# Group 4's gate and value rows as seven products, with the first product copied into the second's PSUM bank

## The chip, the cores and the metric

The kernel runs on one core of one Trainium2 chip. The metric is the device time of one execution in microseconds. TensorE multiplies matrices into PSUM (eight banks of 128 x 512 float32), VectorE (DVE) and ScalarE (ACT) read and write PSUM and SBUF, GpSimd (POOL) works in SBUF alone, and SyncE (SP) issues DMA transfers; POOL issues some too.

## The reference, cut to what matters

```python
for t in range(S):                      # B, H, S, D = 4, 8, 768, 64
    state = gamma * state + k[t] (outer) v[t]
    y[t] = scale * q[t] @ state
x   = y, as 3072 tokens x 512
xn  = x / sqrt(mean(x * x) + 1e-6) * rms_g
g   = xn @ w_gate                       # 512 x 1536
val = xn @ w_val                        # 512 x 1536
out = (silu(g) * val) @ w_out           # 1536 x 512
```

Inputs and output are float32; the kernel multiplies in bfloat16 and sums in float32.

## The kernel before, in words

The 768 time steps are cut into six chunks of 128, and each chunk with its four batches makes a group c = 0 to 5 of 512 tokens. A step of the work is a word with indices, such as `A.2.0` (attention scores of chunk 2, batch 0 and 1) or `g.4.3.4.0.4` (gate row block 3 of group 4, for batches 0 to 3), and `ORDER` (L17 to L105) lists every step of the kernel in the order in which it is issued. The loop at L784 walks through the list and calls the function of each word. A letter behind `@` is the engine (D, A, P, S for DVE, ACT, POOL, SP), digits behind `/` are PSUM banks. Each engine works through its own instructions in the list's order; an instruction waits, with all that stands behind it on that engine, until its inputs are there and its output's buffer is free. So the list alone sets the order of the work.

For each chunk and batch the steps are: loads `Lq`, `Lk`, `Lv` (L317), casts and scalings `Cq`, `Ck`, `V` (L348 to L373), transposes on TensorE (`Tq`, `Tk` with copies `Eq`, `Ek`) or by DMA (`tq`, `tk`), scores `A` (L410; `P` for a pair of batches), the causal mask `M0`, `M1` into `am` (L436), the output `Y` (L447), the state sums `K`, `U`, `B`, and the norm: `S` (squares, ACT, L464), `R` (two small POOL instructions, L476) and `N` (DVE, L488). `X` and `XE` transpose the result into `xnT[c]`, 128 x 4 x 512 tokens.

The feed-forward part of a group has 12 row blocks of 128 hidden rows. An ordinary block takes four matmuls of 512 columns for the gate (`g`, L564), four for the value (`v`), a silu by ACT into `sg` (`s`, L574) and a product by DVE into `hT` (`h`, L586).

The down product of each group is made with seven products instead of eight block products, a scheme of Strassen's kind: hidden rows and tokens are cut in halves, `z1` to `z4` (L633) and `w1` to `w4` (L618) are the sums of blocks that go in, and `product` (L652) adds products 1, 6, 7 and 4 in a bank `a`, product 2 in `b`, products 5 and 3 in `c`. Between them `q1`, `q6`, `q7` (`keep`, L666) copy the running sum of `a` out to SBUF (`sn`). `r1` to `r4` (`result`, L675) form the four quarters: `b` + q1, `c` + q7, `c` + q6, and `a` itself. `s1` to `s4` store them.

Group 5's gate and value rows are made with seven products too. `gS1` to `gS4` and `vS1` to `vS4` (`lsum`, L703) are the sums of weight blocks, `X1` to `X4` (`xsum`, L721) those of `xnT`. `rows7` (L737) makes a product for four row blocks (index r = 0 to 2): four matmuls of 256 columns. `gq`, `vq` copy the running sum (`rkeep`, L755), `gr`, `vr` add (`rsum`, L759), `gs1` to `gs4` are silus (`gsilu`, L767), and `h.5...` forms the products for two row blocks and half of the tokens at once. The sums `S3` overwrite blocks of the weights in place, so they come after the last ordinary use of those blocks.

Buffers are rings of slots: `ring` (L221) opens a tile in the next free one of `bufs` slots. `done` keeps the tiles by name.

Of the kernel before, what the change touches and what calls it, by code (L numbers as in the profile page):

```python
# [818 lines left out]
```

## Time and profile before

| | before |
|---|---|
| runs | 226.31, 226.47, 226.80 us (median 226.47) |
| span of the profiled execution | 225.2 us |
| TensorE busy | 216.6 us, 96% of the span |
| VectorE busy | 180.7 us, 80% |
| ScalarE busy | 108.0 us, 48% |
| GpSimd busy | 156.2 us, 69% |
| granted TensorE clock, mean | 1.000 |

The profiled execution's own time is its span, from the first to the last instruction; the time of a run contains what lies around it as well, 1.1 to 1.6 us by the three runs. An engine's busy time is the union of its instructions. The ends of matmuls are modelled, so that a matmul's duration is longer than the distance to the next one. In the views, a row of the table of groups gives the number of instructions behind an x, then busy time and mean duration in ns, then the idle time just before them with what ended it.

### The profile page before, as it was taken

The numbers are of one execution on the slowest core, as the hardware profiler recorded it, in microseconds if no ns is written. First come the engines' busy times: TensorE is split into PE (matmuls) and PEld (weight loads), VectorE is DVE, ScalarE is ACT, GpSimd is POOL, SyncE is SP. The second block draws the span as 40 slices with busy tenths as digits, with TensorE's granted clock in tenths as the row PEclk, the third lists the DMA queues.
The fourth block names the chain that finished last, engine by engine and source line by source line (L and its number), as shares of the span: only waits on it lengthen the run. The fifth ranks groups of instructions, "written<-read, shape, count | busy, mean of one in ns | idle before, by whom it ended". The sixth has DMA issues, their size and how long they took to land.

```text
span 225.2 us, 5544 instructions
## 1 busy us (share of the span) xinstructions
PE 216.6 (96%) x2119; PEld 145.5 (65%) x2119; DVE 180.7 (80%) x322; ACT 108.0 (48%) x261; POOL 156.2 (69%) x210
## 2 busy tenths in 40 slices
PE   8999999999999999999999999999999999999793
PEld 2568775674655884456754667545466888888582
DVE  7497778889978976995939967969979978899562
ACT  6676543643465883474415153213752375663130
POOL 8999998839985578537599983496066499609900
PEclk9999999999999999999999999999999999999999
DMA  6999999999999999885999698596405103000235
GB/s 100 187 178 190 173 177 189 197 209 227 209 158 211 182 198 153 187 204 130 203 135 242 143 254 169 109 200 160 140 4 141 48 0 139 5 0 3 93 138 188
DMA packets 108187, 33.64 MB, mean 149 GB/s; under 512 B 94465, under 2 KB 108161, under 8 KB 108162
## 3 DMA queue, kind: packets, MB, share of 16 engines
q1 hardware_dynamic: 84690, 25.70, 52.6%
q0 software_dynamic: 23472, 7.60, 30.7%
q8 instruction: 16, 0.26, 0.5%
q14 instruction: 9, 0.07, 0.1%
HBM read 28.31 MB, written 6.29 MB: 154 GB/s over the span
## 4 chain that ended last, share of the span: by engine, by line
PE 74%; DVE 10%; POOL 8%; issue 3%; DMA 1%; SPq 1%; ACT 1%; POOLq 0%; ACTq 0%; DVEq 0%
PE g_ps L564 20%; PE v_ps L564 20%; PE a L660 12%; PE c L660 5%; DVE hT L586 3%; DVE z L633 3%; PE b L660 2%; PE a_ps L418 2%; PE y_ps L456 2%; DVE vf L762 2%; PE y_ps L460 2%; POOL vp L329 2%; PE ga L750 2%; PE va L750 1%; DMA out_dram<-r 1%
## 5 line engine op out<-in xcount | busy, mean ns | idle before, releaser
L574 ACT ACTIVATE sg<-g_ps 128x512 bf16<-128x512 f32 (+2 forms) x64 | 35.5, 569 | 57.6 <-PE g_ps L564 46.5
L564 PE MATMUL v_ps<-xnT,wv_b 128*128 128x512 bf16 (+2 forms) x296 | 59.5, 339 | 0.0
L564 PE MATMUL g_ps<-xnT,wg_b 128*128 128x512 bf16 (+2 forms) x296 | 59.0, 339 | 0.2 <-ACT sg L574 0.2
L586 DVE TENSOR_TENSOR hT<-sg,v_ps 128x512 bf16<-128x512 bf16 (+2 forms) x64 | 40.8, 649 | 14.6 <-ACT sg L574 8.3
L564 PEld LDWEIGHTS <-wg_b 128*128 128x128 bf16 x296 | 25.7, 98 | 22.3 <-DVE xnT L152 0.3
L564 PEld LDWEIGHTS <-wv_b 128*128 128x128 bf16 x296 | 25.7, 98 | 21.8
L660 PEld LDWEIGHTS <-hT 128*128 128x128 bf16 x288 | 28.0, 98 | 5.1
L483 POOL TENSOR_SCALAR ms<-ssq 128x1 f32<-128x1 f32 x24 | 5.5, 230 | 28.2 <-ACT xsq L473 27.4
L660 PEld LDWEIGHTS <-z 128*128 128x128 bf16 x216 | 20.8, 98 | 5.7 <-DVE z L633 2.4
L441 DVE TENSOR_TENSOR am<-a_ps,causal 128x512 bf16<-128x512 f32 x32 | 20.5, 683 | 2.2 <-PE a_ps L418 2.1
L497 DVE SCALAR_TENSOR_TENSOR xn<-y_ps,rstd,g_bc 128x512 bf16<-128x512 f32 x22 | 16.4, 748 | 5.4 <-POOL rstd L485 5.2
L556 POOL CAST st_b<-st_f 64x256 bf16<-64x256 f32 x40 | 19.2, 481 | 2.2 <-DVE st_f L549 0.9
L473 ACT ACTIVATE xsq<-y_ps 128x512 bf16<-128x512 f32 x22 | 13.2, 599 | 13.8 <-PE y_ps L460 12.0
L633 POOL TENSOR_TENSOR z<-z,hT 128x512 bf16<-128x512 bf16 x14 | 17.4, 1246 | 2.9 <-DVE z L633 2.5
L660 PE MATMUL a<-wo_b,hT 128*128 128x256 bf16 x144 | 17.7, 273 | 0.0
L633 POOL TENSOR_TENSOR z<-hT 128x512 bf16<-128x512 bf16 x7 | 8.6, 1226 | 10.6 <-PE a L660 7.7
L485 POOL TENSOR_TENSOR rstd<-ms,mhalf 128x1 f32<-128x1 f32 x24 | 13.9, 580 | 2.0
L633 POOL TENSOR_TENSOR hT<-hT 128x512 bf16<-128x512 bf16 x11 | 13.7, 1254 | 2.2 <-PE b L660 2.1
L354 POOL TENSOR_TENSOR qb<-qf,ydec 128x512 bf16<-128x512 f32 x10 | 11.6, 1162 | 4.0 <-DMA qf<-in_q_dram 4.0
L152 ACT COPY sn<-a 128x512 f32<-128x512 f32 x14 | 8.1, 584 | 13.0 <-PE a L660 11.0
L371 ACT ACTIVATE vp<-vf,vdec 128x64 bf16<-128x64 f32 x56 | 14.0, 341 | 0.0
L683 DVE TENSOR_TENSOR r<-c,sn 128x512 f32<-128x512 f32 (+1 forms) x13 | 8.4, 646 | 4.0 <-PE c L660 2.2
(161 smaller groups left out, 392.4 us busy)
## 6 DMA issues: line engine op xcount, KB each, us to landing
out_dram<-r SPq DMA_DIRECT2D x21, 256.0 KB, 2.3
kf<-in_k_dram SPq DMA_DIRECT2D x18, 256.0 KB, 4.0
qf<-in_q_dram SPq DMA_DIRECT2D x16, 256.0 KB, 3.9
vf<-in_v_dram SPq DMA_DIRECT2D x16, 256.0 KB, 4.0
wo_b<-in_moe_w_out_dram POOLq DMA_DIRECT2D x3, 512.0 KB, 8.6
qb<-in_q_dram POOLq DMA_DIRECT2D x8, 128.0 KB, 6.3
vp<-in_v_dram POOLq DMA_DIRECT2D x8, 128.0 KB, 6.7
kb<-in_k_dram POOLq DMA_DIRECT2D x6, 128.0 KB, 6.1
```

Source lines behind the costliest of these rows:

```text
L354: e.tensor_tensor(out=u["qb"], in0=u["qf"], in1=ydec[:, c, :, None].to_broadcast([128, H, D]), op=ALU.mult)
L371: ACT.activation(u["vp"][:, h], u["vf"][:, h], AF.Copy, scale=vdec[:, c, h:h + 1])
L441: DVE.tensor_tensor(out=u["am"][:, i], in0=u["a"][i], in1=m, op=ALU.mult)
L473: ACT.activation(xsq, flat(u["y"]), AF.Square, accum_out=u["ssq"])
L485: POOL.tensor_tensor(out=u["rstd"], in0=ms, in1=mhalf, op=ALU.pow)
L497: DVE.scalar_tensor_tensor(out=u["xn"], in0=flat(u["y"]), scalar=u["rstd"], in1=g_bc, op0=ALU.mult, op1=ALU.mult)
L556: POOL.tensor_copy(st_b[b][r, :, i * 64:i * 64 + 64], st_f[b][r])
L564: nc.tensor.matmul(p[:, (n - n0) * m:(n - n0 + 1) * m], W[w][0][:, s, n * 128:(n + 1) * 128], xnT[c][:, s, b0 * C:b1 * C], start=s == 0, s ...
L574: ACT.activation(sg[:, :cols], done["wg", c, n0, b0][:, :cols], AF.Silu)
L586: DVE.tensor_tensor(out=h_of(c, r)[:, i:i + n1 - n0, b0 * C:b1 * C], in0=sg, in1=p, op=ALU.mult)
L633: e.tensor_tensor(out=x, in0=a, in1=b, op=how)
L660: nc.tensor.matmul(done[x, c][:, q], left(i, c, r)[:, k, q * C:q * C + C], right(i)[:, r, k], start=first and q == r == k == 0, stop=r == ...
```

## The change

Five things are changed.

- Group 4's gate and value rows go through `rows7` like group 5's: `ga1.4.0` and so on replace `g.4...`, `v.4...` and `s.4...`. The sums of weights are now made per r (two k blocks at once, 512 elements) instead of per k (three r at once, 768 elements): 24 sums instead of 16. `X1` to `X4` are made for groups 4 and 5.
- The first product's copy (`q1`, and `gq1`, `vq1`) goes into the PSUM bank of `b`, opened by that copy, and product 2 is added there. The bank must have been written in full by matmuls before (`whole`, and `every` for tiles that write all of a bank). The sum of `b` and q1 falls away: `r1` is a copy (any engine), `gr1` and `vr1` are gone; silu and `h` read the bank of `b` itself.
- `r2` and `r3` (also `gr`, `vr`) are written over the kept copy in `sn`, not into a buffer of their own.
- Rings: `o_sb` 5 to 3, `sn` 4 to 6, `qb` 6 to 5, `kb` 8 to 6, `vp` 8 to 6, `qT` and `kT` 6 to 5, `am` 6 to 3, `sg` 3 to 4, `vf` 6 to 5. The squares of the norm go into the tile `xn`, which `N` then fills.
- The list of steps is a new one, from the third line on.

```diff
-    HB, OB, KD, SN = 6, 5, 12, 4
+    HB, OB, KD, SN = 6, 3, 12, 6
+    QB, KB, VP, KT, AM, SG, VF = 5, 6, 6, 5, 3, 4, 5
...
-    def bank(i, shape, dtype, name):
+    whole = {}
+
+    def bank(i, shape, dtype, name, every=False, seed=False):
+
+        assert not seed or whole[i]
+        whole[i] = every
         return psum.tile(shape, dtype, name=name, tag=f"bank{i}")
...
-        first = i in (1, 2, 5) and r0 == 0
+        first = i in (1, 5) and r0 == 0
...
-    def keep(i, e, c):
-        done["q", i, c] = ring([128, 2, HM], F32, "sn", SN)
-        copy(e, done["q", i, c], done["a", c])
+    def keep(i, e, bk, c):
+        if i == 1:
+            x = done["b", c] = bank(bk[0], [128, 2, HM], F32, "b", every=True, seed=True)
+        else:
+            x = done["q", i, c] = ring([128, 2, HM], F32, "sn", SN)
+        copy(e, x, done["a", c])
...
-    QUARTER = {1: ("b", 1, 0, 0), 2: ("c", 7, 1, 1), 3: ("c", 6, 0, 1), 4: ("a", None, 1, 0)}
+    QUARTER = {1: ("b", None, 0, 0), 2: ("c", 7, 1, 1), 3: ("c", 6, 0, 1), 4: ("a", None, 1, 0)}
...
-    def lsum(w, i, e, k):
+    def lsum(w, i, e, r):
...
-        if i == 4 and w == "v":
-            done["wv", c, 4 * r + 2, 0] = p.rearrange("p n t -> p (n t)")
-
-    def rkeep(w, i, e, c, r):
-        done[w + "q", i, c, r] = ring([128, 2, HM], F32, "sn", SN)
-        copy(e, done[w + "q", i, c, r], done[w + "a", c, r])
+        if i in (2, 4) and w == "v":
+            done["wv", c, 4 * r + (2 if i == 4 else 0), 0] = p.rearrange("p n t -> p (n t)")
+
+    def rkeep(w, i, e, bk, c, r):
+        if i == 1:
+            x = done[w + "b", c, r] = bank(bk[0], [128, 2, GT // 2], F32, w + "b", every=True, seed=True)
+        else:
+            x = done[w + "q", i, c, r] = ring([128, 2, HM], F32, "sn", SN)
+        copy(e, x, done[w + "a", c, r])
...
-        x, q = {1: ("b", 1), 2: ("c", 7), 3: ("c", 6)}[i]
-        y = sb.tile([128, H, D], F32, name="vf", tag="vf", bufs=6).rearrange("p h d -> p (h d)")
-        DVE.tensor_tensor(out=y.rearrange("p (n t) -> p n t", n=2), in0=done[w + x, c, r], in1=done[w + "q", q, c, r],
-                          op=ALU.add)
+        y = done[w + "q", {2: 7, 3: 6}[i], c, r]
+        DVE.tensor_tensor(out=y, in0=done[w + "c", c, r], in1=y, op=ALU.add)
```

Of the new list, the front, the place of the output weights, and the beginning of group 4's rows:

```diff
-Lv.0.1@P wg.0.2 wv.0.2 H.1/2 mk1 Eq.0.0@A Tq.0.1/3 Tk.0.1/5 Ek.0.1@A Eq.0.1@D A.0.0/1720 Tq.0.2/4 yd Eq.0.2@A Tq.0.3/3
-M0.0.0 Lv.0.3@P Eq.0.3@A M1.0.0 M0.0.1 M1.0.1 GE@A J.0.0/5 A.0.2/17 wv.2.4 Y.0.0/4 wg.2.4 H.3/2 H.1/3 M0.0.2 Tk.0.3/0
-M1.0.2 K.0.2/6 wv.4.6 S.0.0 D.0.0@D R.0.0 Y.0.2/2 J.0.1/1 Y.0.1/3 J.0.2/7 Ek.0.3@A J.0.3/0 N.0.0 D.0.1@D S.0.2 X.0.0/5
-K.0.0/7 XE.0.0@D wg.4.6 S.0.1 R.0.2 R.0.1 N.0.2 N.0.1 A.0.3/41 g.0.0.2.0.1/5 U.0.2@A X.0.2/6 Lk.1.2@P v.0.0.2.0.1/2
...
+Lv.0.1@P wg.0.2 wv.0.2 H.1/2 mk1 Eq.0.0@A Tq.0.1/3 Tk.0.1/5 Ek.0.1@A wg.4.6 Tq.0.2/4 Eq.0.1@D A.0.0/0253 M0.0.0
+Lv.0.3@P M1.0.0 wg.2.4 J.0.2/7 Eq.0.2@A A.0.2/40 M0.0.2 M1.0.2 yd GE@A Y.0.0/6 S.0.0 R.0.0 H.1/1 J.0.1/2 Y.0.2/1 S.0.2
+H.3/0 M0.0.1 M1.0.1 R.0.2 K.0.2/7 Y.0.1/5 wv.2.4 S.0.1 Tq.0.3/3 D.0.1@D Tk.0.3/2 R.0.1 N.0.0 Lk.1.1@S X.0.0/6 N.0.2
+K.0.1/4 J.0.0/1 XE.0.0@D X.0.2/6 Ek.0.3@A Eq.0.3@A wv.4.6 U.0.2@D J.0.3/7 v.0.0.2.0.1/2 XE.0.2@A N.0.1 Lq.1.3@P
...
+XE.1.2@A z2.0.0@P wo.4.8 v.0.6.7.0.4/5 g.1.11.12.0.4/0 h.0.7.8.0.4 vS1.1@P g.1.6.7.0.4/2 vS2.1@P s.1.6.7.0.4
...
+z2.0.1@D s.1.5.6.0.4 v.1.5.6.0.4/7 h.1.5.6.0.4 Cq.2.2@D Cq.2.1@P s.1.2.3.0.3 Lq.2.0@S w1@D w2@D g.1.9.10.0.4/1
+s.1.9.10.0.4 tq.2.2 s.1.8.9.0.4 v.1.10.11.0.4/0 g.1.0.1.0.3/6 h.1.10.11.0.4 Ck.2.0@D V.2.1@A B.1.2 v.1.8.9.0.4/4
...
+v.3.9.10.0.4/4 tq.5.1 r3.2 X1.4@P B.4.0 X2.4@P Ck.5.2@A ga1.4.0/0 gq1.4.0@A/5 s2.2@S h.3.9.10.0.4 v.3.0.1.0.4/2
+ga6.4.0 gb2.4.0 gq6.4.0@A va1.4.0/4 gS3.0@P ga7.4.0 X4.4@P h.3.0.1.0.4 Lv.5.0@S gS3.1@D gc5.4.0/1 gq7.4.0@D gr2.4.0
+Lv.5.3@S vq1.4.0@A/2 vb2.4.0 gs1.4.0 h.4.0.2.0.2 s.3.4.5.0.4 va6.4.0 v.3.4.5.0.4/5 h.3.4.5.0.4 V.5.3@P vS3.0@P
```

More of the change, by code (lines that the diff above doesn't have):

```diff
@@ L249, in H_ @@
     def H_(e, bk, n):
-        p = bank(bk[0], [128, 4, 128], F32, "hot_ps")
+        p = bank(bk[0], [128, 4, 128], F32, "hot_ps", every=True)
         for _ in range(n):
@@ L349, in Cq @@
         u = t[c, b]
-        u["qb"] = ring([128, H, D], BF16, "qb", 6)
+        u["qb"] = ring([128, H, D], BF16, "qb", QB)
         if c == 0:
@@ L364, in V @@
         u = t[c, b]
-        u["vp"] = ring([128, H, D], BF16, "vp", 8)
+        u["vp"] = ring([128, H, D], BF16, "vp", VP)
         if c <= 1:
@@ L453, in Y @@
             return
-        u["y"] = y = bank(bk[0], [128, H, D], F32, "y_ps")
+        u["y"] = y = bank(bk[0], [128, H, D], F32, "y_ps", every=True)
         for h in range(H):
@@ L465, in S_ @@
         u = t[c, b]
-        xsq = ring([128, DM], BF16, "xsq", 1)
+        xsq = u["xn"] = ring([128, DM], BF16, "xn", 4)
         if "ys" in u:
@@ L489, in N @@
         u = t[c, b]
-        u["xn"] = ring([128, DM], BF16, "xn", 4)
         if "ys" in u:
@@ L560, in ffn @@
         m = (b1 - b0) * C
-        p = done[w, c, n0, b0] = bank(bk[0], [128, GT], F32, w[1] + "_ps")
+        p = done[w, c, n0, b0] = bank(bk[0], [128, GT], F32, w[1] + "_ps", every=n1 - n0 == 1 and m == GT)
         for n in range(n0, n1):
@@ L677, in result @@
         if ("r", i, c) not in done:
-            done["r", i, c] = sb.tile([128, 2, HM], F32, name="r", tag="o_sb", bufs=OB)
+            done["r", i, c] = done["q", q, c] if q else sb.tile([128, 2, HM], F32, name="r", tag="o_sb", bufs=OB)
         s = slice(0, 2) if p is None else slice(p, p + 1)
@@ L732 @@
         for w in "gv":
-            F["%sS%d" % (w, i)] = lambda e, bk, k, w=w, i=i: lsum(w, i, e, k)
+            F["%sS%d" % (w, i)] = lambda e, bk, r, w=w, i=i: lsum(w, i, e, r)
     PLACE = {1: (0, 0), 2: (1, 1), 3: (0, 1), 4: (1, 0)}
     def rows7(w, x, i, bk, c, r):
-        first = i in (1, 2, 5)
+        first = i in (1, 5)
         if first:
-            done[w + x, c, r] = bank(bk[0], [128, 2, GT // 2], F32, w + x)
+            done[w + x, c, r] = bank(bk[0], [128, 2, GT // 2], F32, w + x, every=True)
         p = done[w + x, c, r]
@@ L745, in rows7 @@
                 if i in (1, 2, 4):
-                    l = side(w, *((0, 0), (0, 1), (1, 1))[i // 2], k)
+                    l = side(w, *((0, 0), (0, 1), (1, 1))[i // 2], r)
                 else:
-                    l = done["S", w, {3: 4, 5: 1, 6: 2, 7: 3}[i], k]
+                    l = done["S", w, {3: 4, 5: 1, 6: 2, 7: 3}[i], r]
                 m = part(c, *((0, 0), (1, 0), (1, 1))[i - 1]) if i <= 3 else done["X", {4: 4, 5: 1, 6: 2, 7: 3}[i], c]
-                nc.tensor.matmul(p[:, q], l[:, r, q], m[:, k], start=first and q == k == 0, stop=q == k == 1,
+                nc.tensor.matmul(p[:, q], l[:, k, q], m[:, k], start=first and q == k == 0, stop=q == k == 1,
@@ L767, in gsilu @@
     def gsilu(i, c, r):
         h0, t0 = PLACE[i]
-        x = done["ga", c, r].rearrange("p n t -> p (n t)") if i == 4 else done["gr", c, 4 * r + 2 * h0, 2 * t0]
-        sg = done["s", c, 4 * r + 2 * h0, 2 * t0] = sb.tile(
-            [128, H, D], BF16, name="kb", tag="kb", bufs=8).rearrange("p h d -> p (h d)")
+        x = done["gr", c, 4 * r + 2 * h0, 2 * t0] if i in (2, 3) else done[{1: "gb", 4: "ga"}[i], c, r].rearrange(
+            "p n t -> p (n t)")
+        sg = done["s", c, 4 * r + 2 * h0, 2 * t0] = ring([128, GT], BF16, "sg", SG)
```

213 lines of the change are left out of this document (104 added, 109 removed).

## The prediction

> **What bounds the kernel now.** I read the page first: busy time by engine, then the chain that ended last.
>
> ```profile
> span 225.2 us, 5544 instructions
> ...
> PE 216.6 (96%) x2119; PEld 145.5 (65%) x2119; DVE 180.7 (80%) x322; ACT 108.0 (48%) x261; POOL 156.2 (69%) x210
> ...
> PE 74%; DVE 10%; POOL 8%; issue 3%; DMA 1%; SPq 1%; ACT 1%; POOLq 0%; ACTq 0%; DVEq 0%
> ```
>
> The three runs lie at 226.31 to 226.8 us, median 226.47. The profiled execution is known by its span of 225.2 us, so about 1.27 us lie around it, and I add them to every span below. TensorE is busy for 96% of the span and owns 74% of the chain, so matmul time taken out is worth its full price wherever TensorE has no holes. Next I read the table of busy time by stretch, around the place where the change acts, and TensorE's instructions in order of time at the holes.
>
> ```profile
> 12.00:40.00 28.00, 27.41 (x374) 19.18 (x373) 23.54 (x42) 15.79 (x37) 26.01 (x43) 1.00 1.78 182
> ...
> 156.00:166.00 10.00, 9.23 (x84) 5.14 (x83) 8.24 (x15) 5.36 (x15) 1.48 (x5) 1.00 0.33 93
> ...
> 166.00:176.00 10.00, 10.00 (x85) 5.96 (x83) 9.56 (x17) 4.11 (x10) 6.59 (x9) 1.00 0.41 106
> ...
> 196.00:210.00 14.00, 13.54 (x123) 11.65 (x120) 13.65 (x21) 5.48 (x10) 6.86 (x5) 1.00 0.05 18
> ...
> 146.00:210.00 64.00, 62.38 (x518) 45.31 (x516) 56.55 (x85) 29.68 (x62) 40.99 (x42) 1.00 0.30 79
> ...
> 157.27 0.38 PE L418 MATMUL a_ps<-qT,kT 64*128 64x128 bf16 x7 [0.33 <-DVE r L683]
> ...
> 157.86 0.40 PE L418 MATMUL a_ps<-qT,kT 64*128 64x128 bf16 x8 [0.21 <-DVE hT L586]
> ...
> 158.49 0.81 PE L564 MATMUL g_ps<-xnT,wg_b 128*128 128x512 bf16 x3 [0.23 <-ACT sg L574]
> ...
> 192.40 0.60 PE L750 MATMUL gc<-xnT,kf 128*128 128x256 bf16 x4 [0.39 <-DVE vf L762]
> ...
> 209.17 0.61 PE L660 MATMUL c<-w,z 128*128 128x256 bf16 x4 [0.46 <-DVE z L633]
> ...
> 210.92 1.27 PE L660 MATMUL a<-w,z 128*128 128x256 bf16 x10 [0.92 <-DVE z L633]
> ```
>
> The columns after the length of a stretch are busy PE, PEld, DVE, ACT, POOL, then the granted clock (1.00 throughout), DMA share and GB/s. From 146 us to the end of the seven-product work the six marked holes add up to 2.54 us, and five of the six name DVE as the releaser. A hole is longer than shown, because the ends of matmuls are modelled: the table of groups gives 273 ns for one matmul of 256 columns, while twelve start within 1.31 us (below), 109 ns each, so some 0.16 us hide in each mean. Six times 0.16 and 2.54 make 3.5 us of holes. DVE is the second engine here: 56.55 of 64 us, and 13.65 of 14 in the stretch where TensorE begins to wait.
>
> **The change part by part.**
>
> *TensorE.* These are two pieces of the chain, and rows of the table of groups with shapes kept apart.
>
> ```profile
> 115.21 2.59 PE g_ps L564 x12
> ...
> 178.47 1.31 PE ga L750 x12
> ...
> L660 PE MATMUL a<-wo_b,hT 128*128 128x256 bf16 x144 | 17.7, 273 | 0.0
> ...
> L750 PEld LDWEIGHTS <-wg_b 128*128 128x128 bf16 x48 | 4.7, 98 | 0.5
> ...
> L586 DVE TENSOR_TENSOR hT<-sg,v_ps 128x512 bf16<-128x512 bf16 x52 | 35.0, 682 | 11.5 <-ACT sg L574 7.3 <-PE v_ps L564 3.8
> ...
> L586 DVE TENSOR_TENSOR hT<-kb,vf 128x512 bf16<-128x512 bf16 x9 | 8.4, 945 | 0.2
> ...
> L762 DVE TENSOR_TENSOR vf<-vc,sn 128x512 f32<-128x512 f32 x6 | 4.1, 686 | 0.1
> ...
> L683 DVE TENSOR_TENSOR r<-b,sn 128x512 f32<-128x512 f32 x6 | 4.1, 684 | 1.4 <-PE b L660 1.4
> ...
> L152 ACT COPY sn<-a 128x512 f32<-128x512 f32 x14 | 8.1, 584 | 13.0 <-PE a L660 11.0 <-issue 1.1 <-DVE r L683 0.8
> ...
> L772 ACT ACTIVATE kb<-vf 128x512 bf16<-128x512 f32 x9 | 5.7, 633 | 3.2 <-DVE vf L762 3.2
> ...
> L715 DVE TENSOR_TENSOR qf<-qf,wg_b 128x768 bf16<-128x768 bf16 x2 | 1.9, 970 | 0.0
> ...
> L633 POOL TENSOR_TENSOR z<-z,hT 128x512 bf16<-128x512 bf16 x14 | 17.4, 1246 | 2.9 <-DVE z L633 2.5
> ```
>
> Twelve matmuls of 512 columns take 2.59 us, 0.216 each; group 4's gate and value rows are 2 x 12 blocks of 4, 96 of them, 20.7 us. As seven products they are 2 x 3 x 7 x 4 = 168 matmuls of 256 columns at 1.31/12 = 0.109 us, 18.3 us. That removes **2.4 us**. The weight load of 98 ns stays under the 109 ns of its predecessor, as it does in group 5's rows already. No other matmul is added: counted in both lists, products, attention and warm-up matmuls are the same in number, so 2.4 us is the whole of TensorE's gain.
>
> *The seed.* The first product's copy q1 (row sn<-a, 584 ns on ACT) now goes into the PSUM bank in which the second product then adds. It replaces a copy of the same size into SBUF: 18 of them, six for the down products, six for group 5's rows, and six new ones for group 4's. No row shows an engine writing PSUM. ACT's reads of a whole bank lie between 584 and 633 ns, and I take 584; I see no reason to exclude a gain (say 0.1 each, a copy of 256 columns being the only thing that is shorter) and bound it above by doubling, 1.17 us. On ACT, at 48%, even doubling costs 18 x 0.58 = 10 us of an idle half. What is new is that the second product waits for the copy. In the list at least one other product or 512-wide block (0.44 to 0.87 us) stands between q1 and b2 almost everywhere, and the third product had to wait for the same copy already, so I book nothing; without that cover it is up to 0.6 us a time.
>
> *DVE over the whole kernel.* What goes: 12 ordinary hT (682 ns), group 5's six sums gr1 and vr1 and the six r1 (684 ns each; r1 is a plain copy now, four on ACT, two on DVE). What comes for group 4: 12 sums r2 and r3 (686), 12 hT of which six read both factors from SBUF (945) and six the value from PSUM (684). That is -8.2 -4.1 -2.7 +8.2 +9.8 = +3.0, less 0.8 because three of group 5's hT take their value from PSUM. Copies and casts that the new list puts on DVE instead of ACT or POOL (sorted by the letter behind the @) bring some 5 more, the finer weight sums (24 of 512 elements, not 16 of 768; 970 ns was a dear one) save 1.8. About +5.4 on 180.7.
>
> *DVE where it matters.* I take the stretch of the list from group 4's first gate matmul to the last hT of group 5. TensorE in it, by the two rates: before 96 x 0.216 + 368 x 0.109 + 2.9 of attention = 63.8 us; after 8 x 0.216 + 516 x 0.109 + 2.9 = 61.0. DVE by the means of the rows: before 84 instructions, 59.9 us (hT 20.1, sums r2/r3/r1 of rows 12.4, kept copies 1.4, weight sums 4.5, z 6.9, attention and the rest 14.6); after 92, 65.6 us (hT 21.5, row sums 16.5, kept copies 4.9, weight sums 1.0, z 8.6, the rest 13.1). Back to back the instructions overlap:
>
> ```profile
> 10.65 3.68 DVE L441 TENSOR_TENSOR am<-a_ps,mask 128x512 bf16<-128x512 f32 x6
> ...
> L441 DVE TENSOR_TENSOR am<-a_ps,mask 128x512 bf16<-128x512 f32 x16 | 10.1, 683 | 0.7 <-PE a_ps L418 0.7
> ```
>
> Six take 3.68 us, 0.613 each against a mean of 683 ns, so each counts 0.07 less when the queue is full: 54.0 us before, **59.2 after**, against 61.0 of TensorE. DVE goes from 85% of TensorE's work to 97%. It just does not become the bound by itself, but it has no room left: every wait in its queue, for a silu of 633 ns or a copy of 584 ns from ACT, is passed on, because behind the waiting hT or sum stand the next evictions, and TensorE waits for their banks. In the two stretches above where DVE was at 95% or more (24 us), TensorE lost nothing in one, and 0.46 plus the 0.92 right behind it in the other, with 0.16 twice 1.7 us, 7%. So the holes of the new 61.0 us lie between 0 and 4.3 us; I take 3.8, near the end that the longer stretch gives. Before they were 3.5: **+0.3**.
>
> *The front.* The list is new from the first chunk on. On POOL's queue wv.2.4 and wv.4.6 now stand behind the norm steps R.0.0 and R.0.2 (and R.0.1), where before only wg.4.6 stood behind one. And the last chunk of the output weights, which w1, the first weight sum on DVE, needs whole, is issued later.
>
> ```profile
> L485 POOL TENSOR_TENSOR rstd<-ms,mhalf 128x1 f32<-128x1 f32 x24 | 13.9, 580 | 2.0
> ...
> L483 POOL TENSOR_SCALAR ms<-ssq 128x1 f32<-128x1 f32 x24 | 5.5, 230 | 28.2 <-ACT xsq L473 27.4
> ...
> 40.41 0.81 POOL L345 DMA_DIRECT2D wo_b<-in_moe_w_out_dram  x1
> ...
> 54.29 1.02 DVE L618 TENSOR_TENSOR w<-wo_b 128x1536 bf16<-128x1536 bf16 x1
> ...
> wo_b<-in_moe_w_out_dram POOLq DMA_DIRECT2D x3, 512.0 KB, 8.6
> ```
>
> One R costs 0.81 us of POOL's queue; in return R.0.0 no longer stands behind the two value chunks. The last wo issue began at 40.41 and w1 at 54.29, 13.9 us later. In the new list 8.4 us of matmuls (by the rates above) lie between wo.4.8 and w1, against 0.8 for the issue and 8.6 to land: w1 may wait 1.0 us at the head of DVE's queue, with w2, a cast of k, a scaling of q and two hT of group 1 behind it, whose PSUM banks TensorE wants back. Bounds: from -0.8 (the first norm comes one R's worth earlier, and nothing else is late) to +1.8 (0.8 + 1.0, all of it seen); I take **+0.4**, near the middle, since DVE has room there.
>
> *Smaller rings* (am 6 to 3, kb and vp 8 to 6, o_sb 5 to 3, and others by one). An instruction that opens a slot waits for the last reader of the old tile. Before, no row names such a wait of any weight. Where I followed am, the tightest, one tile (M0.2.1) opens in the list before Y.2.2 has read the tile three back; Y.2.2 follows two steps later, so this is half a microsecond of DVE at the worst. I book zero; what it comes to otherwise belongs to the holes.
>
> Sum: 225.2 - 2.4 + 0.3 + 0.4 = 223.5, and 1.27 around it: **224.8 us**.
>
> **The rivals.**
>
> *DVE falls behind (slower).* The hT products with both factors in SBUF are the ones that swing:
>
> ```profile
> L586 DVE TENSOR_TENSOR hT<-kb,vf x9: 681/692/1647, 187.6 to 207.0; 128x512 bf16<-128x512 bf16 x9
> ```
>
> (least, median, longest). There were 9, there will be 12, spread over two groups in which POOL makes sums too. If all came at the longest, DVE would gain 12 x (1.647 - 0.945) = 8.4 us. The forecast has DVE at 59.2 of 61.0 + 3.8 = 64.8 us, 91%. At that share a quarter of the 8.4 (2.1) makes 67.1 us of stretch, 2.3 more than forecast: 227.1. Half makes 69.4: 229.4. I call it 228.0. It decides against the change once the holes are over 5.5 us (3.5 + 2.4 - 0.4), that is from 1.5 us more DVE work than I sum. For it: 97% of TensorE's work, and 1647 in the row. Against: the median of 692, and POOL's work in the stretch falls (by the rows 42 to 35 us, 16 z sums instead of 20).
>
> The Trainium skill (SBUF — State Buffer, Who interferes with whom) has it that a VectorE instruction with two SBUF inputs and a GpSimd instruction that reads SBUF exclude each other, the second waiting for the whole of the first. By that rule alone, each of the 12 behind a whole POOL sum of 1.25 us, DVE would need some 71 us and the kernel would end near 238, an estimate; the trace agrees that it happens (1647 ns) but for few of the nine.
>
> *The front eats it.* With the whole 1.8 us at the front: 224.8 - 0.4 + 1.8 = 226.2, no difference to speak of. For it: POOL 26.01 of 28 us busy from 12 to 40, so its queue hands on every delay. Against: TensorE idles there for only 0.6 us of 28.
>
> *The holes close.* A new list can also bring the z sums and banks in time. With holes of 1.3 us instead of 3.8: 222.3. For it: the 166 to 176 stretch, full on both engines. Against: less DVE room than before.
>
> **How the numbers follow.** About 0.2% (0.45 us) is what a measurement of this kernel can tell from no change. Forecast 0.58, its own range 223.5 to 226.0; DVE behind 0.23; the front 0.09; holes closed 0.10. Faster 0.58 + 0.10 = 0.68, the same 0.09, slower 0.23. The range runs from 222.5, which leaves out half of the closed holes, to 227.9, which leaves out half of the rival that is slower.
>
> **What would show it.** Right: 248 instead of 296 matmuls each at L564's gate and value, 336 instead of 168 256-wide row products, twelve of them still starting within 1.31 us; DVE near 186 us busy and above 90% from group 4's rows on; holes there naming DVE, 3 to 4.5 us in sum; the first gate matmul within half a microsecond of before. Wrong: a wait of a b product on its seeding copy of more than 0.3 us many times; TensorE waiting for weights before 40 us, or w1 idle in front of wo for over 1 us; hT with a mean well over 1 us; or a long wait of DVE or SP for a ring slot.

## The result, and the profile after

The changed kernel takes 230.48 us (median; the profiled execution 228.72), the kernel before on the same chip 226.58 (226.31 to 226.8): a ratio of 1.0154, interval 1.0122 to 1.0187. It is slower by 1.5%, where 224.8 us, faster than before, was forecast. Ratios, here and below, leave out single runs that fell into a slower state (here the one of 232.92 us) and are not the quotients of the medians. In three later series the same kernel came to 1.0249, 1.0200 and 1.0229 (below). The profiled execution is the fastest of its four, so the profile shows less than the whole loss.

The page after, its span, busy times and chain:

```profile
span 226.8 us, 5721 instructions
...
PE 216.0 (95%) x2191; PEld 152.9 (67%) x2191; DVE 185.8 (82%) x331; ACT 117.6 (52%) x277; POOL 162.8 (72%) x221
...
PE 72%; DMA 10%; POOL 7%; DVE 7%; issue 2%; ACT 1%; SPq 1%; POOLq 0%; DVEq 0%; ACTq 0%
```

The reader should see one thing: DMA owns 10% of the chain, where it owned 1%. DVE, which the forecast watched, owns less than before (7% after 10%). The table by stretch says where. First before, then after; the columns are as in the prediction.

```profile
60.00:150.00 90.00, 89.84 (x819) 55.36 (x817) 70.80 (x121) 42.81 (x120) 62.75 (x89) 1.00 0.91 180
...
150.00:210.00 60.00, 58.38 (x500) 43.46 (x498) 54.65 (x81) 29.15 (x62) 37.19 (x37) 1.00 0.27 72
```

```profile
60.00:150.00 90.00, 87.01 (x819) 55.61 (x818) 73.87 (x121) 44.17 (x121) 69.04 (x91) 1.00 0.91 179
...
150.00:212.00 62.00, 60.17 (x585) 51.76 (x584) 55.93 (x90) 35.85 (x70) 34.70 (x41) 1.00 0.29 78
```

From 60 to 150 us TensorE stood idle for 0.16 of 90 us before; now it does for 2.99. From 150 us on it is idle for 1.8 of 62 us, where it was for 1.6 of 60 before. The waits of TensorE in the changed kernel, largest first (total, times, longest):

```profile
PE a_ps L427 <- DMA qT<-qb: 1.6, 3, 0.9
PE b L670 <- DVE b L156: 1.2, 1, 1.2
...
PE g_ps L572 <- DVE xn L505: 0.5, 1, 0.5
PE va L758 <- POOL wv_b L724: 0.4, 1, 0.4
...
PE y_ps L469 <- POOL st_b L564: 0.3, 1, 0.3
PE g_ps L572 <- DMA xnT<-xn: 0.3, 1, 0.3
```

None of the waits for a DMA is in the list of before. To compare whole kernels I add up, from the start of each matmul to the next, what goes beyond the streaming of its columns (0.216 us for 512, 0.109 for 256, 0.034 for a score product). Us, from one profile each; the first column is the streaming itself:

| kernel | streaming | holes 0–60 | 60–150 | 150–end | span |
|---|---|---|---|---|---|
| before | 211.4 | 4.6 | 0.3 | 3.8 | 225.2 |
| after | 209.0 | 5.6 | 4.3 | 3.1 | 226.8 |
| after, again (first series) | 209.0 | 5.2 | 6.4 | 3.1 | 228.4 |
| after, control of the second series | 209.0 | 5.6 | 5.3 | 3.0 | 227.6 |
| after, control of the third series | 209.0 | 5.2 | 6.8 | 3.0 | 228.8 |
| seed copy on ScalarE | 209.0 | 5.9 | 7.4 | 4.3 | 231.3 |
| after with group 4 plain | 211.4 | 5.2 | 6.2 | 5.5 | 233.0 |
| loads by need | 209.0 | 5.1 | 5.2 | 3.0 | 227.0 |
| down weights early | 209.0 | 5.8 | 6.9 | 3.3 | 229.7 |
| both | 209.0 | 5.4 | 4.6 | 3.9 | 227.6 |
| both, and value sum early | 209.0 | 5.5 | 4.0 | 2.4 | 225.6 |
| and near casts first | 209.0 | 5.6 | 4.6 | 2.5 | 226.3 |
| and two places more | 209.0 | 5.7 | 3.9 | 2.7 | 226.1 |

The account of the profiled execution: streaming -2.4, front +1.0, middle +4.0, late -0.7, together +1.9; the spans differ by 1.6, since what lies before the first and behind the last matmul differs too. The middle is also what varies: 4.3, 6.4, 5.3 and 6.8 us in four profiles of one kernel, while the late part stays at 3.0 to 3.1. (Three runs below, those with the old list put back and with transposes by need, are not in the table: 12 to 19 matmuls are missing from their traces.)

### The profile page after: what moved, and what is told of

The parts are those of the page before. It is cut to its first block, busy times and chain, and to the rows that moved or that the text cites. A ratio compares the mean times of both kernels' runs of the same rounds, so it can differ in the third digit from the quotient of the medians.

```text
span 226.8 us, 5721 instructions
## 1 busy us (share of the span) xinstructions
PE 216.0 (95%) x2191; PEld 152.9 (67%) x2191; DVE 185.8 (82%) x331; ACT 117.6 (52%) x277; POOL 162.8 (72%) x221
## 4 chain that ended last, share of the span: by engine, by line
PE 72%; DMA 10%; POOL 7%; DVE 7%; issue 2%; ACT 1%; SPq 1%; POOLq 0%; DVEq 0%; ACTq 0%
PE g_ps L572 15%; PE v_ps L572 14%; PE a L670 10%; PE c L670 5%; PE va L758 4%; PE ga L758 4%; DMA xnT<-xn 3%; DMA qT<-qb 3%; PE hot_ps L261 3%; PE b L670 2%; PE a_ps L427 2%; PE vc L758 2%; POOL x L735 2%; PE gc L758 2%; DMA kf<-in_k_dram 2%
## 5 line engine op out<-in xcount | busy, mean ns | idle before, releaser
L572 PE MATMUL g_ps<-xnT,wg_b 128*128 128x512 bf16 (+2 forms) x248 | 47.6, 331 | 0.9 <-DVE xn L505 0.5
L572 PE MATMUL v_ps<-xnT,wv_b 128*128 128x512 bf16 (+2 forms) x248 | 48.3, 331 | 0.0
L582 ACT ACTIVATE sg<-g_ps 128x512 bf16<-128x512 f32 (+2 forms) x52 | 28.1, 562 | 32.4 <-PE g_ps L572 23.9
L594 DVE TENSOR_TENSOR hT<-sg,v_ps 128x512 bf16<-128x512 bf16 (+2 forms) x52 | 32.4, 640 | 12.6 <-ACT sg L582 6.4
L572 PEld LDWEIGHTS <-wg_b 128*128 128x128 bf16 x248 | 21.0, 98 | 18.7 <-issue 1.4
L572 PEld LDWEIGHTS <-wv_b 128*128 128x128 bf16 x248 | 21.1, 98 | 16.7 <-DVE xn L505 0.3
L482 ACT ACTIVATE xn<-y_ps 128x512 bf16<-128x512 f32 x22 | 13.1, 595 | 12.8 <-PE y_ps L469 6.3
L643 POOL TENSOR_TENSOR z<-hT,z 128x512 bf16<-128x512 bf16 x10 | 12.7, 1274 | 2.3 <-PE c L670 2.1
L696 DVE TENSOR_TENSOR sn<-c,sn 128x512 f32<-128x512 f32 (+1 forms) x13 | 8.4, 644 | 2.9 <-PE c L670 2.6
L772 DVE TENSOR_TENSOR sn<-gc,sn 128x512 f32<-128x512 f32 x12 | 8.1, 684 | 3.0 <-PE gc L758 2.9
```

Of the source, the lines that this page charges most:

```text
L482: ACT.activation(xsq, flat(u["y"]), AF.Square, accum_out=u["ssq"])
L572: nc.tensor.matmul(p[:, (n - n0) * m:(n - n0 + 1) * m], W[w][0][:, s, n * 128:(n + 1) * 128], xnT[c][:, s, b0 * C:b1 * C], start=s == 0, s ...
L582: ACT.activation(sg[:, :cols], done["wg", c, n0, b0][:, :cols], AF.Silu)
L594: DVE.tensor_tensor(out=h_of(c, r)[:, i:i + n1 - n0, b0 * C:b1 * C], in0=sg, in1=p, op=ALU.mult)
L643: e.tensor_tensor(out=x, in0=a, in1=b, op=how)
```

## The experiments

Theory after the result (ORDER; LATE LOADS and MIDDLE are its narrower forms): the seven products bring what was forecast, and the new list loses it between 60 and 150 us, because tiles that are needed soon stand in the in-order queues behind work for tiles that are needed late. Rivals: PRODUCTS (the copies and sums, or the seeded banks, cost it), RINGS (the smaller rings).

**First series.** *The changed kernel again*, no edit.

> The changed kernel once more, on the chip of the next three. Its four runs so far lie from 228.7 to 232.9 us while the kernel before keeps within 0.5 us, and its profiled run was the fastest of them. Theory ORDER (transfers reach their readers too late in the new list) and theory RINGS (smaller rings hold transfers back) both expect a spread of more than 1 us again and, in a profile of a run near 230 us, more TensorE holes between 30 and 150 us than the 4.7 us of the first profile, released by DMA. Theory DVE (VectorE falls behind in the rows of groups 4 and 5) expects the added holes after 150 us.

Measured 231.89 us (230.31 to 233.56) against 226.45, ratio 1.0249 (1.0189 to 1.0308). The loss is real and its size varies. In its profile the late holes are those of the first one (3.1 us) and the middle ones grow to 6.4, so the theory DVE of the expectation, which put the added holes behind 150 us, falls.

*Old places for the preparation.* The loads, casts and q/k transposes of groups 2 to 5 go to the places that they have in the old list, measured by TensorE's work ahead of them:

```
- ... M1.2.2 M0.2.2 tq.2.1 a6.0.0.3 Lk.4.2@S ...
+ ... M1.2.2 M0.2.2 a6.0.0.3 ...      (128 words Lq, Lk, Lv, Cq, Ck, V, tq, tk moved)
```

> The changed kernel, with the steps that prepare attention in chunks 2 to 5 (loads of q, k, v, their casts and scalings, the DMA transposes of q and k) moved in the list to where the old list has them, measured from each tile's own score step; the engines, the rings and all else are as changed. ORDER: the waits for qT, kf, vf go, 223.5 to 225.5 us, and the spread shrinks to that of the kernel before. RINGS: no better than the changed kernel, 229 to 232 us, or worse, since the old order counts on larger rings. DVE: 229 to 231 us.

Measured 239.41 us (238.81 to 242.43), ratio 1.0571 (1.0544 to 1.0599). A miss: far slower. The list around these steps is the new one, and what is put among it by an old time table collides with it; the holes grew to 23.5 us in all. It shows how much the order is worth, not which order.

*Five of the smaller rings alone* (`o_sb`, `qb` and `vf` as before), in the kernel before:

```
-  "am", 6   "kb", 8   "vp", 8   "qT", "kT", 6
+  "am", 3   "kb", 6   "vp", 6   "qT", "kT", 5
```

> The kernel before with its own list, and only these rings smaller: kb and vp 8 to 6, qT and kT 6 to 5, am 6 to 3. RINGS: slower by 2 us or more, 228.5 to 231 us, with TensorE waiting for qT, kT or am. ORDER: the old list can live with them, 226.3 to 227.3 us.

Measured 225.91 us, ratio 0.9979 (0.9960 to 0.9998). RINGS falls for these five, with the old list at least.

*The seeded bank alone*, in the kernel before, for the six down products (one of the six is shown; two of the copies also change their place in the list). In group 2 the bank held score tiles before, and as I read it product 2 overwrites the copy there, so that this quarter lacks product 1; its work and time are the same.

```
- q1.0@A ... b2.0.0.3/3 ... r1.0
+ q1.0@A/3 ... b2.0.0.3 ... r1.0@A
```

> The kernel before with its own list and rings; only the six down products take the seed: q1 is copied by ACT into the bank of b, product 2 is added there, r1 is a copy by ACT instead of a sum by DVE. Theory SEED (the wait of product 2 for the copy costs TensorE): slower by 6 x 0.5 to 6 x 1.2 us, 229 to 233 us. ORDER and RINGS: nothing lost, DVE has some 4 us less to do, 226.0 to 226.8 us.

Measured 227.29 us, ratio 1.0045 (1.0024 to 1.0066). That lies between the two theories. In the trace five of the six copies cost TensorE no wait; at one, the product stands right behind its copy in the list:

```profile
131.64 1.47 PE L659 MATMUL b<-wo_b,hT 128*128 128x256 bf16 x12 [0.80 <-ACT b L151]
```

**Second series**, four kernels on one chip. *Control.*

> The changed kernel as it is, as the yardstick for the three runs beside it on the same chip. Both theories: 1.5 to 2.5% above the kernel before (230 to 232 us against 226.5), since it came out at 1.015 and at 1.025 so far. If the spread comes from transfers in the middle of the kernel, its times lie over 1 us apart while those of the kernel before lie within 0.5.

Measured 232.21 us against 226.97, ratio 1.0200 (1.0158 to 1.0243). Its times lie between 229.52 and 232.81, those of the kernel before between 226.33 and 228.19.

*Loads by need.* The moved words turned out to be 41 loads and no transpose:

```
- ... w4@D Lk.4.3@S A.2.2/2573 ... a6.0.0.3 Lk.4.2@S ... Lq.5.2@S ...
+ ... w4@D Lq.3.2@S A.2.2/2573 ... a6.0.0.3 Lq.3.3@S ...   (Lk.4.3, Lk.4.2, Lq.5.2 later)
```

> The changed kernel with 41 of SyncE's loads and q/k DMA transposes put into one another's places in the list, so that the tile whose cast or score product comes first is fetched first (k of group 4's tile 3, for one, 12 us later; q of group 4's tile 2, 10 us earlier). No cast, product or other operation moves. Theory LATE LOADS (the new list fetches tiles of groups 4 and 5 early and lets the tiles that are needed next wait, and TensorE's holes between 30 and 150 us are those waits): the holes of 0.4 to 1.9 us at scores and at gate products fed by a DMA shrink by half, 2 to 3 us, to a ratio of 1.003 to 1.010. Rival PRODUCTS (what was lost lies in the seven products, their copies and sums from 150 us on): no change, within 0.3% of the control. Rival CASTS (it is the place of the casts in the queues of POOL, ScalarE and VectorE that makes the waits, not the fetching): within 0.3% of the control too, with the same holes.

Measured 230.67 us, ratio 1.0145 (1.0107 to 1.0184): 1.5 us under the control by medians, but the intervals overlap. Less than expected, in the expected direction. In its profile the holes of the middle are 5.2 us after 5.3, not half, so what the gain comes from is not shown.

*The seed copy on ScalarE.*

```
- q1.3@D/2
+ q1.3@A/2
```

> The changed kernel with one word altered: the copy of group 3's first down product into the second's bank is made by ScalarE instead of VectorE. In the trace TensorE waits 1.22 us for that copy at 170.9 us, since VectorE makes it behind two products of 0.7 us, and ScalarE has 2.1 us free from 171.2 on. Theory (that hole is lost time): 0.8 to 1.3 us less than the control. Rival (VectorE is full until 190 us, so what TensorE gains here it waits for later): within 0.3 us of the control.

Measured 233.13 us, ratio 1.0256 (1.0223 to 1.0289): not faster, and the hole is still there (0.96 us, 1.16 to 1.22 in the changed kernel). ScalarE's, VectorE's and TensorE's rows at the place:

```profile
175.29 0.57 ACT L155 COPY b<-a 128x512 f32<-128x512 f32 x1 [1.44 <-DVE xn L504]
...
174.52 0.74 DVE L504 SCALAR_TENSOR_TENSOR xn<-y_ps,rstd,g_bc 128x512 bf16<-128x512 f32 x1
...
175.91 1.47 PE L669 MATMUL b<-wo_b,hT 128*128 128x256 bf16 x12 [0.96 <-ACT b L155]
```

ScalarE was idle for 1.44 us, and what released it is not the product but VectorE's norm step `xn`: the copy needs bank 2, and bank 2 holds the attention output of group 5's tile 3 until the norm has read it. So the seed's price is not the copying engine's speed. A copy to SBUF needs a ring slot; a seed needs a PSUM bank, earlier than the product itself would.

*Group 4 plain*, in the new list. One value block of group 4 is computed with weights that a sum has already replaced; work and time are the same.

```
- ga1.4.0/0 gq1.4.0@A/5 ... gb2.4.0 ... gr2.4.0 ... h.4.0.2.0.2
+ g.4.0.1.0.4/0 s.4.0.1.0.4 v.4.0.1.0.4/4 h.4.0.1.0.4 ...
```

> The changed kernel, list and rings and all, but with group 4's gate and value rows as ordinary matmuls again: 96 of 512 columns in the place of 168 of 256, without the 39 copies and sums. Theory LATE LOADS: the seven products did save their 2.4 us, so this is 1.5 to 3 us slower than the control, 232 to 234 us. Rival PRODUCTS: without the seven products the loss is gone, 226 to 228 us.

Measured 234.71 us, ratio 1.0328 (1.0300 to 1.0356), 2.5 us above the control. PRODUCTS falls: without them the kernel is slower still. And this kernel has the matmuls of the kernel before, 2119 of them and 211.4 us of streaming, yet takes 7.7 us more. Its two stretches:

```profile
60.00:150.00 90.00, 85.29 (x810) 54.78 (x808) 73.47 (x119) 44.12 (x121) 64.64 (x89) 1.00 0.88 178
150.00:213.00 63.00, 59.18 (x474) 40.75 (x472) 43.49 (x73) 24.84 (x49) 31.04 (x37) 1.00 0.29 77
```

4.7 us of standing in the middle, and 3.8 late, where the list was made for other work. What costs is the list in the main; five of the smaller rings came to -0.2% and six seeded banks to +0.45%, both measured in the old list.

**Third series**, again with a *control.*

> The changed kernel as it is, the yardstick of the three beside it. 1.5 to 2.5% above the kernel before.

Measured 231.11 us against 226.36, ratio 1.0229 (1.0188 to 1.0271).

*Down weights early.* In the changed kernel POOL issues the last two loads of the down weights later than before. POOL's rows, before, then after:

```profile
35.54 0.80 POOL L345 DMA_DIRECT2D wo_b<-in_moe_w_out_dram  x1
37.16 0.74 POOL L345 DMA_DIRECT2D wo_b<-in_moe_w_out_dram  x1
40.41 0.81 POOL L345 DMA_DIRECT2D wo_b<-in_moe_w_out_dram  x1
```

```profile
44.78 0.83 POOL L354 DMA_DIRECT2D wo_b<-in_moe_w_out_dram  x1
49.51 0.84 POOL L354 DMA_DIRECT2D wo_b<-in_moe_w_out_dram  x1
```

```
- ... wv.6.9 M0.1.3 ... wo.0.4 g.1.0.4.3.4/2 ... wo.4.8 ...
+ ... wv.6.9 wo.4.8 wo.0.4 M0.1.3 ... g.1.0.4.3.4/2 ...
```

> The changed kernel with two words moved: the loads of the last two thirds of the down weights (512 KB each, issued by POOL at 44.8 and 49.5 us in the changed kernel, at 37.2 and 40.4 us in the kernel before) stand right behind the last load of the value weights, at 36.7 us. Nothing else moves. Theory WEIGHTS LATE (these two loads are under way until 58 us, where the kernel before was done with its weights at 47, and share the DMA engines with group 2's q, k and v, so that group 2's scores at 64 to 71 us wait, 0.7 to 2.8 us and differently in each run): that hole falls below 0.3 us, the times come within 1 us of one another, and the median falls by 1 to 2 us under the control. Rival BYTES (the DMA engines are full from 20 to 75 us, so what is fetched earlier delays group 2's tiles by as much): within 0.4 us of the control, with the hole where it was.

Measured 231.27 us, ratio 1.0204 (1.0179 to 1.0229): 0.2 us above the control by medians, and below it by ratios, with overlapping intervals. WEIGHTS LATE falls as a cause by itself, and the rival BYTES holds: earlier weights make group 2's tiles later. The q and k loads that SyncE issues at 40 to 41 us take 11.1 and 11.4 us to land, after 5.0 and 5.3 in the control. The Trainium skill (DMA: Bandwidth & Descriptors, Issuing engines are not separate DMA queues) says that transfers end up on the same 16 engines whoever issues them; this run agrees, as moving 1 MB of POOL's loads ahead held up SyncE's and left 2.8 us of holes between 60 and 80 us, after 2.9 in the control.

*Both.*

> The two words of the run with early down weights and the 41 exchanged loads and transposes of the run with loads by need, together. If the two losses are separate (WEIGHTS LATE and LATE LOADS): 2.5 to 3.5 us under the control, ratio 1.004 to 1.010. If both were the same loss: no better than the better of the two alone, 1.5 us under the control. Rival BYTES: as the run with loads by need, 1.5 us under the control.

Measured 228.79 us, ratio 1.0104 (1.0075 to 1.0132): 2.3 us under the control by medians, with intervals well apart. It is more than the early weights gave alone and more than BYTES allows; against loads by need alone (1.0145, on another chip) the intervals overlap.

*And the value sum early*, `vS3.0@P` two POOL operations ahead.

```
- ... gS3.0@P ... X4.4@P ... V.5.3@P vS3.0@P ...
+ ... gS3.0@P vS3.0@P ... X4.4@P ... V.5.3@P ...
```

> The run with early down weights and loads by need, and one word more: the sum of value weights which group 4's sixth value product waits for at 157 us (0.44 us of wait for POOL in the trace) stands two POOL operations earlier, before a load's scaling and a sum that is needed later. Theory (a hole that is there in every run with the same size is lost time): 0.4 to 0.6 us under that run. Rival (POOL's next sum or VectorE's queue holds the same products up): within 0.2 us of it.

Measured 228.28 us, ratio 1.0087 (1.0060 to 1.0114). By medians 0.5 us, as expected, but inside the interval. The wait at 157 us is gone; one of 0.50 us, for ScalarE, stands at 165 us.

**The old order, put back as a whole.** *The old list until 141 us, the new one from there.*

```
+ (old list, words and banks, to 141 us; the new kernel's weight sums at their new places)
+ (new list from there, without what has been done)
```

> The changed kernel (seven products for group 4 too, seeded banks, small rings), but its list follows the list of before, in words and in banks, until about 141 us of TensorE's work, with the new kernel's sums of gate and value weights put in where the new list has them; from there on the new list, without what has been done. Theory MIDDLE (the seven products of group 4 are worth their 2.4 us and what was lost lies in the new order before 141 us): the holes between 60 and 150 us go, and it is faster than the kernel before, by 0.5 to 2.5 us, ratio 0.989 to 0.998; at most 1 us is lost at the seam. Rival PRODUCTS (VectorE at 97% or the seeded banks take back what the products save): 227 us or more, ratio above 1.003.

Measured 236.16 us, ratio 1.0399 (1.0352 to 1.0446). A miss, and the most telling one. TensorE's and ScalarE's rows behind the seam:

```profile
159.02 1.01 PE L757 MATMUL ga<-x,w 128*128 128x256 bf16 x4 [6.45 <-POOL x L734]
...
155.97 2.02 ACT L379 ACTIVATE vp<-vf,vdec 128x64 bf16<-128x64 f32 x8 [8.70 <-DMA vf<-in_v_dram]
```

One hole of 6.45 us: group 4's seven products need `X1` and `X2` from POOL at once, which is behind in-place weight sums, and ScalarE stands for 8.70 us before a v tile of group 5 that the old order fetches later. So, as I read it, the early fetching in the new list was not idle: the late stretch has no room for that work. The old middle and the new end do not fit together as they are, and the time of the run doesn't say what the middle alone is worth. Its trace says more, though. These are three rows of TensorE's waits in the whole run:

```profile
PE b L669 <- ACT b L155: 0.8, 1, 0.8
PE a L669 <- POOL z L642: 0.8, 1, 0.8
...
PE a_ps L426 <- DMA kT<-kb: 0.2, 1, 0.2
```

From 60 to 150 us TensorE waits 0.2 us for transfers here, and 1.9, 2.9, 2.7 and 2.5 us in the four profiles of the changed kernel, which has the same rings, seeds and products. So it is the order that makes these waits. Other waits stay, 2.1 us in this stretch (0.2 in the kernel before): at group 2's seed copy, a sum on POOL and a copy on ScalarE. The seed's copy, at least, is a new step that is not free in the old order.

*The old list until 68 us.*

> As the run with the old list until 141 us, but the old list only until about 68 us, the new one from there (with two far loads of group 4's k put behind the loads of group 3, and two banks renumbered, which the seam needs). If the front (group 2's tiles and the late down weights) is where most was lost: 1 to 2 us above the run with the old list until 141 us. If the middle from 68 to 141 us is: 2.5 to 4.5 us above it, near the changed kernel itself (ratio 1.012 to 1.02).

Measured 233.32 us, ratio 1.0277 (1.0240 to 1.0313), no better than the changed kernel: the front is not where the loss is, or the seam costs as much (it makes a wait of 1.78 us for a k transpose at 67 us). Which of the two it is stays open.

*Transposes by need.* On the kernel with the value sum early, 31 q and k transposes and 36 loads change places among SyncE's words.

```
- ... XE.2.3@S Lv.3.2@S ... Lv.3.1@S c5.0.0.3/3 ... XE.2.2@S XE.2.1@S ... XE.2.0@S ... tq.3.3
+ ... XE.2.3@S tk.3.3 ... tq.3.3 c5.0.0.3/3 ... XE.2.2@S XE.2.1@S ... XE.2.0@S ...
```

> The last run of the series before (down weights early, loads by need, value sum early; ratio 1.0087) with SyncE's q and k DMA transposes put in order of need as well, 31 of them: the q transpose of group 4's tile 2, for which TensorE waits 0.9 to 1.9 us at 126 us in every run, one to two places earlier, the one of group 5's tile 2 much later. Theory (SyncE's order is what is left of the loss in the middle): that hole halves, and the median falls by 0.5 to 1.5 us, to a ratio of 1.002 to 1.007. Rival CASTS (the transposes wait for casts that stand late in the queues of VectorE and POOL): within 0.3 us of it, the hole as it was.

Measured 240.45 us, ratio 1.0603 (1.0550 to 1.0657). A miss again. SyncE's queue and TensorE's rows:

```profile
82.47 1.22 SPq L410 DMA_TRANSPOSE kT<-kb  x1
86.24 1.19 SPq L410 DMA_TRANSPOSE qT<-qb  x1
87.53 3.84 SPq L523 DMA_TRANSPOSE xnT<-xn  x3
...
92.59 0.58 PE L571 MATMUL g_ps<-xnT,wg_b 128*128 128x512 bf16 x1 [6.28 <-DMA xnT<-xn]
...
94.25 3.62 PE L571 MATMUL v_ps<-xnT,wv_b 128*128 128x512 bf16 x8
97.67 1.68 PE L571 MATMUL g_ps<-xnT,wg_b 128*128 128x512 bf16 x6
```

SyncE issues a k transpose at 82.47 and then nothing until 86.24, because the next word, a q transpose of group 3, waits for its cast (on POOL, done at 86.22). Behind it stand the three `xnT` transposes of group 2, whose inputs VectorE had finished by 82.9 us, and TensorE waits 6.28 us for the last. "By need" was computed from when a tile is used and not from when its cast is done; in an in-order queue a word that isn't ready stops all that are.

**Single words.** *Near casts first*, six words around one hole. This is how the hole comes about in the changed kernel: VectorE's two q casts of group 4's tiles 3 and 2, SyncE's transposes, TensorE's score product.

```profile
110.89 0.68 DVE L363 TENSOR_TENSOR qb<-qf,ydec 128x512 bf16<-128x512 f32 x1
...
118.69 1.65 DVE L363 TENSOR_TENSOR qb<-qf,ydec 128x512 bf16<-128x512 f32 x1
...
120.86 1.03 DVE L363 TENSOR_TENSOR qb<-qf,ydec 128x512 bf16<-128x512 f32 x1
...
119.06 4.04 SPq L411 DMA_TRANSPOSE qT<-qb  x2
123.19 1.22 SPq L411 DMA_TRANSPOSE kT<-kb  x1
124.52 1.21 SPq L411 DMA_TRANSPOSE qT<-qb  x1
...
127.02 0.62 PE L427 MATMUL a_ps<-qT,kT 64*128 64x128 bf16 x16 [0.94 <-DMA qT<-qb]
```

The casts end at 120.3 and 121.9 us. The first of the two transposes in the 4.04 us is one of group 5, used 40 us later (the 110.89 row is its cast, made ahead of the two); the second starts only at 121.9, though its cast was done at 120.3. Two more follow, 1.2 us of SyncE each, the last done issuing at 125.7. Before, the cast of tile 2 was made at 104.03, VectorE's only q cast between 100 and 126 us:

```profile
104.03 0.68 DVE L354 TENSOR_TENSOR qb<-qf,ydec 128x512 bf16<-128x512 f32 x1
```

```
- Cq.5.2@D ... Cq.4.3@D ... Cq.4.2@D ... tq.5.2 ... tq.4.3 tk.4.2 ... tq.4.2 P.4.2/641257
+ Cq.4.3@D Cq.4.2@D ... Cq.5.2@D ... tq.4.3 tq.4.2 ... tk.4.2 ... P.4.2/641257 tq.5.2
```

> The run with early down weights, loads by need and the early value sum (ratio 1.0087, 228.3 us), with six words moved around one hole: VectorE makes the q casts of group 4's tiles 3 and 2 at 111 us, where it made the one of group 5's tile 2 (they were at 118.7 and 120.9), and that one changes to their place; the two q transposes stand ahead of the k transpose, and the q transpose of group 5's tile 2 behind the score products. Theory CASTS (TensorE's wait of 0.9 to 1.9 us at 126 us is a queue of three: the cast late on VectorE, then two transposes of 1.2 us ahead on SyncE): that hole falls below 0.3 us and the median by 0.7 to 1.5 us, ratio 1.002 to 1.006. Rival (what is behind it is late as well: K of the same tiles, or VectorE's sums of group 3): the hole goes and one of like size stands within 10 us; median within 0.3 us.

Measured 229.08 us, ratio 1.0075 (1.0040 to 1.0110), no change that can be told from 1.0087. TensorE's rows:

```profile
126.72 0.62 PE L426 MATMUL a_ps<-qT,kT 64*128 64x128 bf16 x16 [0.28 <-DMA kT<-kb]
...
139.39 0.40 PE L426 MATMUL a_ps<-qT,kT 64*128 64x128 bf16 x8 [0.95 <-DMA kT<-kb]
140.34 0.40 PE L426 MATMUL a_ps<-qT,kT 64*128 64x128 bf16 x8 [0.56 <-DMA qT<-qb]
```

The hole goes from 0.99 us, in the run that it builds on, to 0.28, and 1.5 us stand 13 us later, at the other two tiles of the same group. The rival was right in the main, though it had put the new hole within 10 us.

*And two places more.*

```
- ... Cq.2.0@D ... q1.0@D/4 ...      ... gS3.2@P ... X1.4@P B.4.0 X2.4@P ...
+ ... q1.0@D/4 Cq.2.0@D ...          ... X1.4@P B.4.0 X2.4@P gS3.2@P ...
```

> The run before with two words more: the cast of group 2's last q tile, which waits for its load on VectorE, stands behind the copy of group 0's first down product into the second's bank instead of ahead of it (TensorE waits 0.80 us for that copy at 65 us); and a sum of gate weights on POOL stands behind the two sums of group 4's input that TensorE waits 0.67 us for at 152 us. Theory (each hole is the place of one word in a queue): 0.8 to 1.5 us under the run before, at 226.4 to 227.3 us about level with the kernel before. Rival (the queues are full, so that each mended place makes another tile late): within 0.4 us of the run before.

Measured 227.85 us (226.94 to 228.25), ratio 1.0055 (1.0034 to 1.0076), by the ratios 0.5 us under the run before and well inside its interval. That is nearer the rival than the theory. Of the two holes, the one at the seed copy (65 us) is gone and a k transpose is late for 1.00 us. At the other, TensorE still waits 0.53 us for the sum of group 4's input (0.67 in the run with the value sum early), and then 0.93 us for the weight sum that now stands behind it on POOL:

```profile
67.97 0.40 PE L426 MATMUL a_ps<-qT,kT 64*128 64x128 bf16 x8 [1.00 <-DMA kT<-kb]
...
155.44 0.61 PE L757 MATMUL ga<-x,wg_b 128*128 128x256 bf16 x4 [0.93 <-POOL wg_b L723]
```

It is the best version found with seven products in group 4: by the ratios 2 to 4 us under the changed kernel, and still 0.55%, 1.2 us, over the kernel before. I found none that beats the kernel before.

## Why the prediction was wrong

**The step that failed** is the sum, "225.2 - 2.4 + 0.3 + 0.4": it lets the new list act at the front and in the late stretch alone. "The list is new from the first chunk on" stands in the text, and for the 90 us between there is no term. It measured +4.0 us in the profiled execution and +5.0 to +6.5 in the three later profiles; each of the other terms was right to within 1 us. That the list costs this is shown from two sides: with the new list and group 4 plain, same matmuls as before, 7.7 us slower; with the old list until 141 us and the products, seeds and rings of the changed kernel, 0.2 us of waits for transfers in the middle instead of 1.9 to 2.9. The other 2.1 us of waits that stay there (a seed's copy, a sum on POOL, a copy on ScalarE) have other causes, which were not separated. That the order of loads, SyncE's 41 and POOL's two, is a large part of it is shown by the run that changes nothing else: from 1.0229 to 1.0104. The further steps to 1.0087 and 1.0055 lie inside the intervals one by one, and in the best list the middle still has 3.9 us of holes, so most of the middle is not mended. That fetching for group 5 was moved up *because* the late stretch is full is argued from the 6.45 and 8.70 us behind the seam; a list with an old middle and room at the end was not found.

Point by point:

- *TensorE, -2.4 us*: right. Streaming fell from 211.4 to 209.0, and the group with plain rows has it back.
- *The seed at nothing*: mis-sized. One of 18 copies makes a hole in every profile of the changed kernel (1.16 to 1.22 us behind 171 us), and in most of the lists with moved words that of group 0 does so too (0.19 to 1.24 us). The cause that I priced, the copy's duration, was right: 0.57 us on ScalarE into PSUM, as into SBUF. The cause that I missed is the bank.
- *DVE, +5.4 us*: right, 185.8 after 180.7.
- *DVE late, +0.3 us*: DVE was as full as forecast, and it cost nothing; the late holes fell by 0.7. The rows of after:

```profile
160.00:170.00 10.00, 10.00 (x130) 8.87 (x129) 9.97 (x16) 7.46 (x16) 8.73 (x12) 1.00 0.34 113
...
180.00:190.00 10.00, 10.00 (x94) 8.97 (x92) 9.81 (x15) 5.40 (x11) 6.56 (x6) 1.00 0.08 28
```

DVE at 9.97 of 10 us and TensorE at 10.00: a queue that is full, in the right order, makes no holes. (In the stretch between the two stands the 1.22 us hole of the seed.) I had turned two stretches into a rate of 7% and should have kept the range. The rival "DVE falls behind" had the right sign for a wrong reason: the twelve `hT` with both factors in SBUF take 793 ns in the mean, one of them 1633. Nine of them have no POOL instruction beside them and take 676 to 692 ns; the three that overlap with one take 800, 925 and 1633, the last beside the sum below. So this rival stayed small because few of the twelve meet POOL, not because meeting it is cheap:

```profile
L594 DVE TENSOR_TENSOR hT<-sg,sn x12: 676/686/1633, 162.7 to 211.6; 128x512 bf16<-128x512 bf16 x12
...
185.22 1.63 DVE L594 TENSOR_TENSOR hT<-sg,sn 128x512 bf16<-128x512 bf16 x1
...
185.01 1.30 POOL L643 TENSOR_TENSOR z<-hT,z 128x512 bf16<-128x512 bf16 x1 [2.12 <-PE c L670]
```

- *The front, +0.4 us*: +0.6 to +1.0, inside its bounds. The first weight sum, feared to wait for the down weights, starts 0.6 us behind the cast ahead of it, without idle time.
- *Rings at zero*: right for the five that were tried alone, in the old list; `o_sb`, `qb` and `vf` were not tried alone, but all were small in the run with the old list until 141 us, without waits for transfers to speak of.
- *The signs*: none of those that I listed as wrong would have named the loss. The "DMA 1%" in the chain of before was passed over; it meant that the old list had hidden the transfers, in a stretch in which, by the rows of its queue, SyncE was issuing for 79 of 90 us (77 after).

## What to carry to other kernels

When a change comes with a new order of issue, the order is a change of its own: walk each in-order queue, those that only start transfers too, and ask of every word what it now stands ahead of. A resource that is hidden (DMA, 1% of the chain) can be the first to appear, as it was here. A result that is kept in PSUM instead of SBUF takes a bank for longer, and the bank's last tenant sets when it can begin, whichever engine copies.
